# Attention scores as float32 products of q and k as loaded, with two buffers each for the loads of k and v

## The chip, the cores and the metric

The kernel runs on one core of one Trainium2 chip. The metric is the device time of one execution in microseconds; the median of three runs is quoted. The trace is one further execution, recorded by the hardware profiler.

## What is computed

An attention layer with a compressive memory, and behind it a feed-forward block (FFN) with a squared ReLU. `B, H, S, D = 4, 8, 576, 64`, so 2304 tokens of width 512; the hidden width is 2048. All inputs are float32.

```python
scores = where(causal, -1e9, q @ k.T / sqrt(D))
a = softmax(scores);  local = a @ v
q_p = phi(q)                                   # phi(x) = where(x > 0, x, exp(x) - 1) + 1
mem_out = (q_p @ M_prev) / (q_p @ z_prev + 1e-6)
g = sigmoid(beta)                              # one for each head
x = (g * mem_out + (1 - g) * local)            # heads side by side: 2304 x 512
out = (maximum(x @ w_in, 0) ** 2) @ w_out      # the FFN
```

## The kernel before

**The work.** The first 64 tokens of each batch are done together at the start (`first_tokens`). The remaining 512 queries of a batch are four tiles of 128 rows (tiles 1 to 4). A *unit* is one batch, one pair of heads and a list of tiles: batches 0 and 1 are cut into a low half (tiles 1, 2) and a high half (tiles 3, 4), batches 2 and 3 are not, which gives 24 units (0 to 23), numbered in the order in which they are traced. The 9 FFN blocks of 256 tokens are `moe(0)` to `moe(8)`; `moe(0)` has the first tokens, `moe(n)` a half of a batch. Attention outputs go to DRAM (`xd`, L567), and `prefetch` reads them back as `xn` (L588), transposes them (L591) and splits them into a rounded and a remainder part, `xh` and `xl`. The FFN multiplies with three float32r products for each pair of operands (L624 to L626, L614 to L616). The weights are loaded and split into `hi` and `lo` at the start (L160 to L166, loads in L190).

**A unit.** `loads` brings `kd` (both heads' k, transposed, 128 x 576), `qm` (memory matrix and q, two buffers) and `vv` (v), all on SP's queue. `kd` and `vv` have one buffer each (`KB`, `VVB`). For units 6 to 23, ScalarE (ACT) rounds q and k to float32r (`qh` L359, `kh` L364), and the remainders `ql` and `kl` are formed on VectorE (DVE) (L360, L365), or on GpSimd (POOL) for `kl` of units 6 to 11. The scores of a strip are then three products (`qh kh`, `ql kh`, `qh kl`) for each of the two heads, which lie on different halves of the array's rows. Units 0 to 5 (`NES`) multiply `qm` and `kd` themselves in float32; the trace shows two records for each such product. Strips have 192 (tile 1), 320 (tile 2), 448 (tile 3) and twice 288 columns (tile 4); tile 2 comes first (`TORD`). A single PSUM tile `sp` takes a strip of both heads. L465 on DVE adds the mask, writes `e` and takes the row minimum of the negated scores; L477 on ACT is the exponential. For units 0 and 1 the weights `e` are transposed on PE and multiplied with `vv` itself (L535). For all later units `e` is split into two float16 parts (L514, L516), transposed by a DMA (`aT`, L520) and multiplied with `vs` (L541 to L546). `vs` is `vv` scaled by a power of two that comes from its maximum `vx` (L393 to L403) and split into two float16 parts (L408, L410), after which `vv` is free.

**phi.** `pe`, the exponential of q, takes a slot of the ring `e` of three buffers. Units 6 to 23 write q's relu over q (L376) and join both on DVE (L377); units 0 to 5, whose q is still wanted by PE, take the minimum with 1 on POOL (L382) and join on DVE (L383). `pm` (L428) multiplies phi(q) with the memory matrix.

**The order of the work.** The program is traced unit by unit; next to the first four units stand the weights and `moe(0)`, and `moe(1)` to `moe(8)` are traced last. A scheduler of the language then orders each engine's instructions when the kernel is built: it takes the earliest traced instruction that its own model of time has ready, and allots the buffers. On the chip every engine and every DMA queue goes through its list in order, and instructions wait by semaphores. So the FFN matmuls fill PE where attention has nothing ready.

Of the kernel before, what the change touches and what calls it, by code (L numbers as in the profile page):

```python
# [8 lines left out]
F32 = mybir.dt.float32  # L9
F32R = mybir.dt.float32r  # L10
# [3 lines left out]
AF = mybir.ActivationFunctionType  # L14
ALU = mybir.AluOpType
AX = mybir.AxisListType

B, H, S, D = 4, 8, 576, 64
# [3 lines left out]
P = 128  # L22
# [6 lines left out]
SQ = S - D  # L29
# [4 lines left out]
SC = 16384.0  # L34
VEXP = 14
VL = 'dd'
PM = 'pd'
FX = 'dd'
GHN = 4
VMIN = 2.0**-80  # L40
NEF = 2
NES = 6
PXT = 'up'
PXE = 'aa'
PHI = 1
QB = 2
VVB = 1
ZW = D + 1
MW = 576
WSC = 1.0 / 256.0  # L50
EB = 3
RB = 1
KB = 1
XB = 2
PJ = 6
SEQ = 'a0 b0 g a1 r b1 r c0 l r r c1'
W0 = 9
EARLY = 'dp'
LATE = 'dd'
NEARLY = 12  # L60
SEG = 2
TORD = [2, 1, 3, 4]
# [25 lines left out]
def fused_kernel(ctx: ExitStack, tc: tile.TileContext, t0_d, zt_d, kk_d, qv_d, beta, w_in, w_out, out):  # L88
    nc = tc.nc
# [3 lines left out]
    at = ctx.enter_context(tc.tile_pool(name="at", bufs=1))  # L93
# [13 lines left out]
        out=mask, in_=mask, pattern=[[-1, MW]], compare_op=ALU.is_ge, fill=-1e30, base=448, channel_multiplier=1  # L107
# [219 lines left out]
    dp = ctx.enter_context(tc.tile_pool(name="dp", bufs=1, space=bass.MemoryType.DRAM))  # L327
# [12 lines left out]
        nc.sync.dma_start(vv[:, :nv], qv_d[b, p, :, SQ + 2 * ZW : SQ + 2 * ZW + nv])  # L340
        return kd, qm, vv

    def attention(b, p, tiles, ld, after, early, sfull, full):
        q_eng, k_eng = (nc.gpsimd if c == 'p' else nc.vector for c in (EARLY if early else LATE))
        late = 0 if early else 1
        h0 = 2 * p
        tl = tiles[-1]
        kn, ncn = sum(QT[tl]), tl + 1
        qa, qb = QT[tiles[0]][0] - D, kn - D
        kd, qm, vv = ld  # L350
        q_raw = qm[:, 2 * ZW :]
        mz = qm[:, : 2 * ZW]
        v = vv.rearrange("p (c x) -> p c x", c=5)
        heads = [slice(h * D, (h + 1) * D) for h in range(2)]

        if not sfull:
            qh, ql = (at.tile([P, SQ], F32R, tag=t, name=t) for t in ("qh", "ql"))
            kh, kl = (at.tile([P, S], F32R, tag=t, name=t) for t in ("kh", "kl"))
            nc.scalar.copy(qh[:, qa:qb], q_raw[:, qa:qb])  # L359
            q_eng.tensor_tensor(  # L360
                out=ql[:, qa:qb], in0=q_raw[:, qa:qb], in1=qh[:, qa:qb].bitcast(F32), op=ALU.subtract
            )
            yield
            nc.scalar.copy(kh[:, :kn], kd[:, :kn])  # L364
            k_eng.tensor_tensor(out=kl[:, :kn], in0=kd[:, :kn], in1=kh[:, :kn].bitcast(F32), op=ALU.subtract)  # L365
            yield
            terms = [(qh, kh), (ql, kh), (qh, kl)]
        else:
            terms = [(q_raw, kd)]

        pe = at.tile([P, 2, S], F32, tag="e", name="pe", bufs=EB)[:, 0]
        w = slice(qa, qb)
        nc.scalar.activation(pe[:, w], q_raw[:, w], AF.Exp)
        ph = pe if sfull else q_raw
        if PHI and not sfull:
            nc.scalar.activation(q_raw[:, w], q_raw[:, w], AF.Relu)  # L376
            nc.vector.scalar_tensor_tensor(  # L377
                out=q_raw[:, w], in0=pe[:, w], scalar=1.0, in1=q_raw[:, w], op0=ALU.min, op1=ALU.add
            )
        else:  # L380
            m_eng = nc.gpsimd if PM[late] == "p" else nc.vector
            m_eng.tensor_scalar(out=pe[:, w], in0=pe[:, w], scalar1=1.0, scalar2=None, op0=ALU.min)  # L382
            nc.vector.scalar_tensor_tensor(  # L383
                out=ph[:, w], in0=q_raw[:, w], scalar=0.0, in1=pe[:, w], op0=ALU.max, op1=ALU.add
            )
        yield

        if not full:
# [11 lines left out]
                out=vy, in0=vy, scalar1=VMIN, scalar2=2.0**-VEXP, op0=ALU.max, op1=ALU.mult  # L400
# [6 lines left out]
            if VL[late] == "d":  # L407
                nc.scalar.activation(vh, vr, AF.Copy, scale=vy)  # L408
                for h in range(2):
                    nc.vector.scalar_tensor_tensor(  # L410
                        out=vl[:, h], in0=vr[:, h], scalar=vy, in1=vh[:, h], op0=ALU.mult, op1=ALU.subtract
# [8 lines left out]
        for grp in (tiles[:2], tiles[2:]):  # L420
# [4 lines left out]
            for j, i in enumerate(grp):  # L425
# [6 lines left out]
                out=nm[:, :ng], in0=pv[:, :, :, D], scalar=1e-6,  # L432
# [14 lines left out]
        for i in [t for t in TORD if t in tiles]:  # L447
# [8 lines left out]
            for s in range(ns):  # L456
                ks = slice(s * w, (s + 1) * w)
                sps = ps.tile([P, 2, 512], F32, tag="s", name="sp")
                for x, (qt, kt) in enumerate(terms):
                    for h, hd in enumerate(heads):  # L460
                        nc.tensor.matmul(  # L461
                            sps[:n, h, :w], qt[hd, qc], kt[hd, ks], start=x == 0, stop=x == len(terms) - 1
                        )
                for h in range(2):
                    nc.vector.tensor_tensor_reduce(  # L465
                        out=e[:n, h, ks],
                        in0=sps[:n, h, :w],
                        in1=mask[:n, 448 - q0 + s * w : 448 - q0 + s * w + w],
                        scale=-0.125,
                        scalar=3e38 if s == 0 else mx[:n, h, 0:1],  # L470
                        op0=ALU.add,
                        op1=ALU.min,
                        accum_out=mx[:n, h, s : s + 1],
                    )
# [229 lines left out]
    def attn(i0, i1):  # L704
        for i in range(i0, i1):
            ld = nxt.pop()

            def after():
                if i + 1 < len(order):
                    nxt.append(loads(*order[i + 1]))  # L710

            yield from attention(*order[i], ld, after, i < NEARLY, i < NES, i < NEF and max(order[i][2]) < 4)

    def na(t):
        return NP * (6 + (len(t) > 3) + 2 * len(t) - 1)
# [64 lines left out]
```

## Time and profile before

| | |
|---|---|
| median of 3 runs | 610.11 us (610.11 to 610.82) |
| profiled execution: time, span | 609.23 us, 607.4 us |
| PE busy (matmul) | 569.1 us, 94% |
| DVE, ACT, POOL busy | 411.2 us (68%), 329.0 us (54%), 170.3 us (28%) |
| mean granted TensorE clock | 0.986 of full speed |
| chain that ended last | PE 63%, DVE 13%, DMA 9%, ACT 9% |

The span runs from the first to the last instruction, and the execution's time lies around it. PE's busy time is made of modelled matmul durations that overlap, so a busy PE is not PE at its peak; what a matmul costs is better read from the distance between starts.

### The profile page before, as it was taken

What the parts mean: (1) busy time and instruction counts of PE and PEld (TensorE: products, weight loads), DVE (VectorE), ACT (ScalarE), POOL (GpSimd) and SP (SyncE); (2) the same over time, 40 slices, a digit from 0 to 9 for tenths busy, and PEclk for the clock granted to TensorE, in tenths of its full rate; (3) what the DMA queues carried; (4) which work ended last, traced back from release to release, by engine and by line L of the source; (5) the groups of instructions that cost most, each with busy time, mean ns of one, the idle gap of its engine ahead of it and who ended that gap; (6) DMA issues with size and microseconds to landing.
All of it is one profiled execution on the core that took longest, in us unless ns stands there. A gap on an engine that the chain in (4) does not pass through costs nothing.

```text
span 607.4 us, 11542 instructions
## 1 busy us (share of the span) xinstructions
PE 569.1 (94%) x4198; PEld 482.7 (79%) x4198; DVE 411.2 (68%) x1285; ACT 329.0 (54%) x747; POOL 170.3 (28%) x139
## 2 busy tenths in 40 slices
PE   2479997999989999999999999999999999999997
PEld 2358876787868787888888888888888899998996
DVE  5999798868677879887888978788697711001000
ACT  3689686756566664775576645654556413312312
POOL 2501232134423233233332233232321121221221
PEclk9989998999997999999999999999999999999999
DMA  8947575673574775664655564575435510100000
GB/s 278 402 144 301 165 210 159 139 169 85 117 165 111 160 155 129 145 173 88 164 115 114 145 126 107 114 167 118 103 70 119 99 24 2 68 1 1 36 1 35
DMA packets 127576, 76.28 MB, mean 126 GB/s; under 512 B 99360, under 2 KB 112672, under 8 KB 127520
## 3 DMA queue, kind: packets, MB, share of 16 engines
q1 hardware_dynamic: 127520, 75.55, 49.7%
q8 instruction: 33, 0.54, 0.4%
q14 instruction: 23, 0.19, 0.1%
HBM read 42.63 MB, written 8.78 MB: 85 GB/s over the span
## 4 chain that ended last, share of the span: by engine, by line
PE 63%; DVE 13%; DMA 9%; ACT 9%; issue 3%; SPq 1%; POOL 1%; ACTq 0%
PE up L624 9%; PE up L626 8%; PE up L625 8%; PE oacc L614 8%; PE oacc L616 8%; PE oacc L615 8%; PE sp L461 6%; DMA aT<-a 3%; DMA vv<-in_qv_dram 3%; ACT e L477 2%; PE acc L546 2%; DVE a L516 2%; PE pm L428 2%; DVE e L465 2%; DVE memx L556 2%
## 5 line engine op out<-in xcount | busy, mean ns | idle before, releaser
L624 PE MATMUL up<-xh,w 128*128 128x256 f32 x576 | 167.0, 290 | 3.4 <-ACT aF L496 2.5
L626 PE MATMUL up<-xh,w 128*128 128x256 f32 x576 | 166.1, 288 | 0.0
L625 PE MATMUL up<-xl,w 128*128 128x256 f32 x576 | 165.9, 288 | 0.0
L639 POOL TENSOR_TENSOR gl<-r,gh 128x512 fp32r<-128x512 f32 x72 | 98.9, 1373 | 203.6 <-DVE gh L638 124.4
L624 PEld LDWEIGHTS up<-xh,w 128*128 128x128 f32 x576 | 111.2, 193 | 10.9 <-issue 3.9
L614 PE MATMUL oacc<-w,gh 128*128 128x512 f32 x288 | 116.0, 403 | 3.6 <-ACT gh L636 3.5
L625 PEld LDWEIGHTS up<-xl,w 128*128 128x128 f32 x576 | 111.3, 193 | 5.2 <-issue 2.5
L615 PE MATMUL oacc<-w,gh 128*128 128x512 f32 x288 | 114.4, 397 | 0.0
L626 PEld LDWEIGHTS up<-xh,w 128*128 128x128 f32 x576 | 111.2, 193 | 3.4 <-issue 2.2
L477 ACT ACTIVATE e<-e,mx 128x320 f32<-128x320 f32 (+3 forms) x128 | 77.8, 609 | 65.4 <-DVE mx L465 65.0
L616 PE MATMUL oacc<-w,gl 128*128 128x512 f32 x288 | 111.7, 403 | 0.0
L516 DVE SCALAR_TENSOR_TENSOR a<-e,a 128x128 f16<-128x128 f32 x120 | 79.4, 677 | 19.8 <-ACT a L514 19.6
L630 ACT ACTIVATE r<-up 128x512 f32<-128x512 f32 x72 | 42.4, 590 | 92.5 <-PE up L626 86.6
L632 POOL TENSOR_TENSOR r<-r 128x512 f32<-128x512 f32 x40 | 46.5, 1162 | 164.1 <-ACT r L630 164.1
L638 DVE CAST gh<-r 128x512 fp32r<-128x512 f32 x40 | 16.9, 423 | 87.9 <-ACT r L634 86.4
L614 PEld LDWEIGHTS oacc<-w,gh 128*128 128x128 f32 x288 | 54.5, 189 | 15.7 <-ACT gh L636 4.0
L616 PEld LDWEIGHTS oacc<-w,gl 128*128 128x128 f32 x288 | 53.2, 189 | 13.5 <-issue 3.8
L465 DVE CUSTOM_DVE_ANT_0 e<-sp,mask 128x320 f32<-128x320 f32 (+3 forms) x128 | 56.2, 475 | 9.0 <-PE sp L461 8.9
L615 PEld LDWEIGHTS oacc<-w,gh 128*128 128x128 f32 x288 | 54.5, 189 | 9.4 <-issue 0.9
L514 ACT ACTIVATE a<-e 128x128 f16<-128x128 f32 x120 | 56.9, 521 | 5.7 <-DMA aT<-a 4.7
L548 DVE TENSOR_REDUCE s<-acc 128x128 f32<-128x256 f32 x60 | 24.0, 417 | 21.2 <-PE acc L546 21.2
L546 PE MATMUL acc<-vs,aT 128*128 128x128 f16 x308 | 37.4, 222 | 0.0
(127 smaller groups left out, 883.4 us busy)
## 6 DMA issues: line engine op xcount, KB each, us to landing
raw<-in_w_in_dram SPq DMA_DIRECT2D x11, 512.0 KB, 7.9
vv<-in_qv_dram SPq DMA_DIRECT2D x16, 320.0 KB, 2.8
raw<-in_w_out_dram SPq DMA_DIRECT2D x9, 512.0 KB, 7.8
kd<-in_kk_dram SPq DMA_DIRECT2D x16, 288.0 KB, 3.1
out_dram<-o SPq DMA_DIRECT2D x16, 256.0 KB, 2.0
xd<-memx SPq DMA_DIRECT2D x31, 128.0 KB, 2.1
xn<-xd SPq DMA_DIRECT2D x14, 256.0 KB, 3.2
qm<-in_qv_dram SPq DMA_DIRECT2D x8, 321.0 KB, 2.9
```

Of the source, the lines that this page charges most:

```text
L465: nc.vector.tensor_tensor_reduce(out=e[:n, h, ks], in0=sps[:n, h, :w], in1=mask[:n, 448 - q0 + s * w : 448 - q0 + s * w + w], scale=-0.125 ...
L477: nc.scalar.activation(e[:n, h, :ke], e[:n, h, :ke], AF.Exp, bias=bs, scale=-1.0, accum_out=sm[:n, h : h + 1])
L514: nc.scalar.mul(av[:, :, o0 : o0 + w], x, SC)
L516: nc.vector.scalar_tensor_tensor(out=av[:, :, o0 + w : o0 + 2 * w], in0=x, scalar=SC, in1=av[:, :, o0 : o0 + w], op0=ALU.mult, op1=ALU.sub ...
L546: nc.tensor.matmul(o2, aT[:, h * nb + c, :n], vs[:, h, c], start=False, stop=c == i)
L614: nc.tensor.matmul(acc[t], gh[:, u, ts], w_out_op(f, 0), start=f == 0, stop=False)
L615: nc.tensor.matmul(acc[t], gh[:, u, ts], w_out_op(f, 1), start=False, stop=False)
L616: nc.tensor.matmul(acc[t], gl[:, u, ts], w_out_op(f, 0), start=False, stop=f == NF - 1)
L624: nc.tensor.matmul(up[:, u, :], w_in_op(f, k, 0), xh[:, k, :], start=k == 0, stop=False)
L625: nc.tensor.matmul(up[:, u, :], w_in_op(f, k, 0), xl[:, k, :], start=False, stop=False)
L626: nc.tensor.matmul(up[:, u, :], w_in_op(f, k, 1), xh[:, k, :], start=False, stop=k == NK - 1)
L639: nc.gpsimd.tensor_tensor(out=gl, in0=r, in1=gh.bitcast(F32), op=ALU.subtract)
```

## The change

All units multiply `q_raw` and `kd` in float32, so `qh`, `ql`, `kh` and `kl` go away with the four instructions that write them. phi is formed for all units from two tiles of its own, `ph` (two buffers) and `pr` (one), with exponential and relu on ACT and the join on DVE; `pe` no longer takes a slot of the ring `e`. `kd` and `vv` get a second buffer. The number of buffers of `qm` stays 2.

```diff
-VVB = 1
+VVB = 2
-KB = 1
+KB = 2
-        if not sfull:
-            qh, ql = (at.tile([P, SQ], F32R, tag=t, name=t) for t in ("qh", "ql"))
-            kh, kl = (at.tile([P, S], F32R, tag=t, name=t) for t in ("kh", "kl"))
-            nc.scalar.copy(qh[:, qa:qb], q_raw[:, qa:qb])
-            q_eng.tensor_tensor(
-                out=ql[:, qa:qb], in0=q_raw[:, qa:qb], in1=qh[:, qa:qb].bitcast(F32), op=ALU.subtract
-            )
-            yield
-            nc.scalar.copy(kh[:, :kn], kd[:, :kn])
-            k_eng.tensor_tensor(out=kl[:, :kn], in0=kd[:, :kn], in1=kh[:, :kn].bitcast(F32), op=ALU.subtract)
-            yield
-            terms = [(qh, kh), (ql, kh), (qh, kl)]
-        else:
-            terms = [(q_raw, kd)]
-
-        pe = at.tile([P, 2, S], F32, tag="e", name="pe", bufs=EB)[:, 0]
         w = slice(qa, qb)
-        nc.scalar.activation(pe[:, w], q_raw[:, w], AF.Exp)
...
+        ph = at.tile([P, SQ], F32, tag="ph", name="ph", bufs=2)
+        pr = at.tile([P, SQ], F32, tag="pr", name="pr", bufs=1)
+        nc.scalar.activation(ph[:, w], q_raw[:, w], AF.Exp)
+        nc.scalar.activation(pr[:, w], q_raw[:, w], AF.Relu)
+        nc.vector.scalar_tensor_tensor(
+            out=ph[:, w], in0=ph[:, w], scalar=1.0, in1=pr[:, w], op0=ALU.min, op1=ALU.add
+        )
...
-                for x, (qt, kt) in enumerate(terms):
-                    for h, hd in enumerate(heads):
-                        nc.tensor.matmul(
-                            sps[:n, h, :w], qt[hd, qc], kt[hd, ks], start=x == 0, stop=x == len(terms) - 1
-                        )
+                for h, hd in enumerate(heads):
+                    nc.tensor.matmul(sps[:n, h, :w], q_raw[hd, qc], kd[hd, ks], start=True, stop=True)
```

## Rows read from the trace of the kernel before

**Rows 1.** Busy time of each engine in four stretches of the span: stretch and its length, then busy us and instructions of PE, PE's weight loads, DVE, ACT and POOL, granted clock, DMA share and GB/s.

```profile
0.00:131.00 131.00, 102.97 (x728) 84.30 (x729) 113.01 (x329) 91.98 (x210) 33.20 (x32) 0.96 0.71 221
131.00:200.00 69.00, 64.39 (x490) 53.87 (x488) 54.12 (x185) 41.77 (x107) 26.18 (x22) 0.95 0.56 122
200.00:479.00 279.00, 276.96 (x2166) 231.45 (x2165) 228.85 (x736) 161.45 (x374) 82.94 (x65) 1.00 0.57 126
479.00:607.40 128.40, 124.80 (x821) 113.11 (x819) 15.19 (x37) 33.82 (x58) 27.94 (x22) 1.00 0.10 30
```

**Rows 2.** Waits of PE between 131 and 200 us: the instruction that waited, what it waited for, us in total, times, longest.

```profile
PE px L591 <- DMA xn<-xd: 2.1, 1, 2.1
PE acc L541 <- DMA aT<-a: 1.0, 1, 1.0
```

**Rows 3.** The stretch behind the read of `xn`, columns as in rows 1.

```profile
175.00:182.00 7.00, 4.33 (x42) 3.36 (x40) 5.72 (x25) 4.07 (x13) 0.86 (x1) 0.97 0.77 208
182.00:189.00 7.00, 6.89 (x34) 5.89 (x33) 5.50 (x25) 3.40 (x11) 0.00 (x0) 0.54 0.45 100
```

**Rows 4.** PE's instructions in order of time: whole groups of scores and the instruction behind each. `kd` operands are the float32 groups, `kh` and `kl` the float32r ones.

```profile
71.93 0.28 PE L626 MATMUL up<-xh,w 128*128 128x256 f32 x1
72.14 0.81 PE L461 MATMUL sp<-kd,qm 64*128 64x320 f32 x4
72.88 0.39 PE L624 MATMUL up<-xh,w 128*128 128x256 f32 x1
...
113.28 1.02 PE L461 MATMUL sp<-kd,qm 64*128 64x448 f32 x4
114.24 0.39 PE L624 MATMUL up<-xh,w 128*128 128x256 f32 x1
...
131.27 0.48 PE L461 MATMUL sp<-kh,qh 64*128 64x448 f32 x2
...
132.08 0.39 PE L625 MATMUL up<-xl,w 128*128 128x256 f32 x1
...
163.99 0.42 PE L461 MATMUL sp<-kh,qh 64*128 64x320 f32 x2
...
164.63 0.39 PE L624 MATMUL up<-xh,w 128*128 128x256 f32 x1
```

**Rows 5.** The scores' matmuls of L461, one term of the float32r groups: count, shortest, median and longest ns, first and last start, and the shapes.

```profile
L461 PE MATMUL sp<-kh,qh x132: 353/398/632, 131.3 to 477.3; 64*128 64x288 f32 x56, 64*128 64x448 f32 x28, 64*128 64x320 f32 x24, 64*128 64x192 f32 x24
```

**Rows 6.** PE's instructions in order of time: the first and the last of the 21 float32r groups that are cut by other work (the first between the heads, the last between the terms), and one of those between.

```profile
155.71 0.40 PE L461 MATMUL sp<-kh,qh 64*128 64x288 f32 x2
...
173.33 0.42 PE L461 MATMUL sp<-kh,qh 64*128 64x320 f32 x2
...
173.83 0.73 PE L616 MATMUL oacc<-w,gl 128*128 128x512 f32 x2
...
176.32 0.41 PE L461 MATMUL sp<-kl,qh 64*128 64x320 f32 x2
176.66 0.23 PE L541 MATMUL acc<-vs,aT 128*128 128x128 f16 x1
...
456.19 0.41 PE L461 MATMUL sp<-kh,qh 64*128 64x320 f32 x2
```

**Rows 7.** The same view: the one float32 group that is cut between its heads, first head.

```profile
87.48 1.02 PE L461 MATMUL sp<-kd,qm 64*128 64x448 f32 x2
88.43 0.50 PE L614 MATMUL oacc<-w,gh 128*128 128x512 f32 x1
```

**Rows 8.** Groups of instructions by line: count, busy us and mean ns of one, and the engine's idle time before them with what ended it.

```profile
L364 ACT CAST kh<-kd 128x576 fp32r<-128x576 f32 (+1 forms) x18 | 11.2, 622 | 28.2 <-PE sp L461 28.2
L376 ACT ACTIVATE qm<-qm 128x256 f32<-128x256 f32 (+1 forms) x18 | 9.0, 503 | 0.2 <-DVE ql L360 0.2
L359 ACT CAST qh<-qm 128x256 fp32r<-128x256 f32 (+1 forms) x18 | 8.9, 496 | 0.6 <-DMA qm<-in_qv_dram 0.6
L360 DVE TENSOR_TENSOR ql<-qm,qh 128x256 fp32r<-128x256 f32 (+1 forms) x18 | 13.2, 733 | 0.4 <-ACT qh L359 0.3
L365 DVE TENSOR_TENSOR kl<-kd,kh 128x576 fp32r<-128x576 f32 x12 | 9.0, 750 | 0.0
L365 POOL TENSOR_TENSOR kl<-kd,kh 128x320 fp32r<-128x320 f32 (+1 forms) x6 | 7.4, 1225 | 15.7 <-ACT kh L364 15.7
L382 POOL TENSOR_SCALAR pe<-pe 128x256 f32<-128x256 f32 x6 | 6.3, 1057 | 31.4 <-ACT pe L373 31.0 <-PE acc L535 0.4
```

**Rows 9.** The chain of work that ended last, in order of time: start, us, what.

```profile
142.87 3.28 DMA vv<-in_qv_dram
```

**Rows 10.** SP's queue in order of time, ahead of the read of `xn` for the second block: start, us of the issue, what.

```profile
175.95 0.52 SPq L340 DMA_DIRECT2D vv<-in_qv_dram  x1
...
177.00 0.90 SPq L588 DMA_DIRECT2D xn<-xd  x2
```

**Rows 11.** SP, ACT and PE in order of time around the last weight loads.

```profile
84.62 0.33 SPq L340 DMA_DIRECT2D vv<-in_qv_dram  x1
86.19 0.33 SPq L190 DMA_DIRECT2D hw<-in_w_out_dram  x1
...
90.80 0.69 ACT L161 ACTIVATE hw<-hw 128x512 f32<-128x512 f32 x1 [2.79 <-DMA hw<-in_w_out_dram]
...
101.91 0.50 PE L614 MATMUL oacc<-w,gh 128*128 128x512 f32 x1 [3.51 <-ACT gh L636]
```

More of the change, by code (lines that the diff above doesn't have):

```diff
@@ L36 @@
 VL = 'dd'
-PM = 'pd'
 FX = 'dd'
@@ L41 @@
 NEF = 2
-NES = 6
 PXT = 'up'
 PXE = 'aa'
-PHI = 1
 QB = 2
-VVB = 1
+VVB = 2
 ZW = D + 1
@@ L57 @@
 W0 = 9
-EARLY = 'dp'
-LATE = 'dd'
 NEARLY = 12
@@ L341, in loads, with attention @@
         return kd, qm, vv
-    def attention(b, p, tiles, ld, after, early, sfull, full):
-        q_eng, k_eng = (nc.gpsimd if c == 'p' else nc.vector for c in (EARLY if early else LATE))
+    def attention(b, p, tiles, ld, after, early, full):
         late = 0 if early else 1
@@ L354, in attention @@
         heads = [slice(h * D, (h + 1) * D) for h in range(2)]
-        if not sfull:
-            qh, ql = (at.tile([P, SQ], F32R, tag=t, name=t) for t in ("qh", "ql"))
-            kh, kl = (at.tile([P, S], F32R, tag=t, name=t) for t in ("kh", "kl"))
-            nc.scalar.copy(qh[:, qa:qb], q_raw[:, qa:qb])
-            q_eng.tensor_tensor(
-                out=ql[:, qa:qb], in0=q_raw[:, qa:qb], in1=qh[:, qa:qb].bitcast(F32), op=ALU.subtract
-            )
-            yield
-            nc.scalar.copy(kh[:, :kn], kd[:, :kn])
-            k_eng.tensor_tensor(out=kl[:, :kn], in0=kd[:, :kn], in1=kh[:, :kn].bitcast(F32), op=ALU.subtract)
-            yield
-            terms = [(qh, kh), (ql, kh), (qh, kl)]
-        else:
-            terms = [(q_raw, kd)]
-        pe = at.tile([P, 2, S], F32, tag="e", name="pe", bufs=EB)[:, 0]
-        w = slice(qa, qb)
-        nc.scalar.activation(pe[:, w], q_raw[:, w], AF.Exp)
[L374 to L378, printed above, removed]
-            )
[L380 to L385, printed above, removed]
+        w = slice(qa, qb)
+        ph = at.tile([P, SQ], F32, tag="ph", name="ph", bufs=2)
[5 more added lines that the diff above has]
+        )
         yield
@@ L458, in attention @@
                 sps = ps.tile([P, 2, 512], F32, tag="s", name="sp")
-                for x, (qt, kt) in enumerate(terms):
-                    for h, hd in enumerate(heads):
-                        nc.tensor.matmul(
-                            sps[:n, h, :w], qt[hd, qc], kt[hd, ks], start=x == 0, stop=x == len(terms) - 1
-                        )
+                for h, hd in enumerate(heads):
+                    nc.tensor.matmul(sps[:n, h, :w], q_raw[hd, qc], kd[hd, ks], start=True, stop=True)
                 for h in range(2):
@@ L710, in after @@
                     nxt.append(loads(*order[i + 1]))
-            yield from attention(*order[i], ld, after, i < NEARLY, i < NES, i < NEF and max(order[i][2]) < 4)
+            yield from attention(*order[i], ld, after, i < NEARLY, i < NEF and max(order[i][2]) < 4)
     def na(t):
```

## The prediction

> **What bounds the kernel now.** I read the busy shares by stage first [rows 1]. Until 131 us no engine is full: PE is busy 102.97 of 131 us, DVE 113.01. From 200 to 479 us PE is busy 276.96 of 279 us, and after that 124.80 of 128.4. So from 200 us on the time is the sum of PE's work: a microsecond added to PE there is a microsecond of the span, and one taken from DVE or ACT is worth nothing by itself. Between the two lies 131 to 200 us, where PE idles 4.6 us (69.00 less 64.39) although the FFN block has work queued. The waits of PE in that stretch name it: the read of the next block's tokens, `xn`, and the transposed weights `aT` [rows 2]. Behind the `xn` wait the granted clock fell too: 0.54 of full speed over the 7 us from 182 to 189 us, after PE had been busy for only 4.33 of the 7 us before, so some 3.2 us more of work were lost there ((1 - 0.54) x 7) [rows 3]. In all 7.8 us are to be had in this stretch, and 2.0 after it up to 479 us.
>
> **The fourth pass, on PE.** Units 0 to 5 already multiply in float32, units 6 to 23 with three float32r products, so both prices stand in the trace. I take a group (both heads of one strip of scores) from its first start to the start of the next instruction. With 320 columns float32 takes 72.88 - 72.14 = 0.74 us, with 448 columns 0.96; float32r takes 0.64 and 0.81 [rows 4]. Per column that is (0.96 - 0.74) / 128 = 1.7 ns against (0.81 - 0.64) / 128 = 1.3 ns; on these lines 288 columns cost 0.69 and 0.60, 192 columns 0.52 and 0.47. Units 6 to 23 have 66 groups: 12 with 192 columns, 28 with 288, 12 with 320, 14 with 448 [rows 5], the instructions of one term halved for the two heads. With whole groups on both sides the change adds 12 x 0.05 + 28 x 0.09 + 12 x 0.10 + 14 x 0.15 = 6.4 us.
>
> But the float32r groups aren't whole. Going through PE's timeline I count 21 of the 66 that are cut by other work, 18 of them between terms (scores start on `kh` and `qh`, and `kl` or `ql` comes later) and 3 between the heads; first and last stand in [rows 6]. A cut is dear, since every group has two edges: it starts 0.09 us late (71.93 + 0.12, the step of these matmuls, is 72.05, and the group starts at 72.14), and the matmul behind it lasts 0.39 instead of 0.28 [rows 4]. Edges are 0.20 us in all. The 320-column group at 173.33 takes 0.50 and, at 176.32, 0.34 more; against a whole one of 0.64 that is 0.20, and the second pair of edges makes 0.40 a cut. 21 x 0.40 = 8.4 us. Float32 operands come straight from the load, so there is no late term to cut at: only the cut between heads stays. One of the 14 float32 groups was cut so, and each head alone took 0.95 us [rows 7], as much as both together, so this cut costs 0.95 + 0.95 - 0.96 + 0.20 = 1.1 us. At 3 to 5 of 66 that is 3 to 6 us; I take 5. PE's sum: 6.4 - 8.4 + 5 = +3 us, between -2 (none cut) and +6.4 (the cuts of before come back in some other place, so that nothing is saved).
>
> The Trainium skill, in FP8 and Floating Point Precision (TensorE Precision Notes), says that true float32 goes through the array in four passes. The trace agrees, at 1.7 ns a column against 1.3 for three. By the pass count alone this speaks against the change; it is a rival below, and the sum here doesn't use it.
>
> **What goes from ACT, DVE and POOL.** Four instructions a unit for 18 units: the casts `kh` and `qh` (11.2 + 8.9 us of ACT), `ql` and `kl` (13.2 + 9.0 of DVE, 7.4 of POOL) [rows 8]. From 200 us on PE covers all of it, so I book nothing there. With `kh` goes ACT's wait for its single buffer: 28.2 us in which ACT stood until PE had done the last scores of the unit before [rows 8]. PE covers that too. The second exponent buffers `ph` and `pr` replace a slot of the `e` ring; the same PSUM and the same instructions on DVE remain. In units 0 to 5 POOL's minimum (6 x 1.06 us) becomes a relu on ACT; the nearest rows are the relu of the later units, 0.50 us a piece over both widths [rows 8], so up to 6 x 0.50 = 3.0 us if all six lie on the path, none if POOL's step was the longer way round. I take 0.5.
>
> **The second buffers.** A unit's `vv` may now be loaded before the unit before has scaled its own. At 142.87 us the chain of work that ended last goes through this load, 3.28 us [rows 9]; the load stood for the slot that VectorE frees, and in VectorE's order the maximum `vx` of the loaded tile stands ahead of an `a` and with it the `aT` transposes that PE waits for. Gone is thus one reload in each unit on the chain, and for units 6 and 7 the kl of POOL on top. SP's queue has the same wait in front of other work: the `xn` read was issued at 177.00 us, behind a `vv` load at 175.95 which stood for the scaling [rows 10]. Between them lies a `qm` load, which may keep some of the 1.05 us: it needs the last scores of two units earlier now, because `q` is read by PE itself; the transposes and the `xn` read queue behind it on SP, and PE waits for both. `pr` has one buffer, which VectorE frees after one instruction; I book nothing for it, since the next relu is a whole unit later. The second `kd` buffer buys nothing new: it stands in for `kh` and `kl`, since `kd` is now held until the last scores.
>
> What is that worth? At least nothing: `aT` (a DMA after the slowest DVE step) and the round trip of `xd` and `xn` stay. At most the 7.8 us. The attention of units 4 to 7 has to end some 4 us earlier for PE not to run dry; two reloads of about 3 us and the split of units 6 and 7 are more than that, if VectorE follows. I take 5.5 of the 7.8.
>
> Before 131 us `vv` loads stand ahead of weight loads in SP's queue as well: issued at 84.62, followed by a weight load at 86.19 for which ACT then waits 2.79 us at 90.80, and PE stands 3.51 us at 101.91 for ACT [rows 11]. So 0 to 3.5 us; DVE is busy almost throughout, so I take 1.5.
>
> **Sum.** 3 (PE) + 0.5 (relu) - 5.5 (131 to 200 us) - 1.5 (early) = -3.5 us. The profiled execution has a span of 607.4 us and a time of 609.23; 605.7 for this one's time. The median of the runs shown is 610.11, 0.9 above it, so I predict 606.6.
>
> **The rivals.**
> *A: the fourth pass is paid and nothing comes back* (slower). The extra pass counts on PE after 200 us, where nothing hides it, at 6.4 us, and the stall before the second block only changes its name: `aT` and `xn` are still late, because DVE, not the load, sets them. Plus the relu, 0 to 3: 616.5 to 619.5; with half of the stalls recovered 613. For it: PE is 99% busy there. Against it: 21 cuts are in the rows, and their cause is removed. It decides where PE's extra is larger than the stalls recovered. Counted in passes alone the price is higher: one more for 20,480 columns (12 x 192 + 28 x 288 + 12 x 320 + 14 x 448) at 1.3 / 3 = 0.43 ns is 8.9 us, and 610.11 + 8.9 = 619. The Trainium skill's FP8 and Floating Point Precision gives this count. The whole groups of [rows 4] lie less far apart than that, 0.10 us at 320 columns where a pass is 0.14. Together 0.27.
> *B: no difference* (608.9 to 611.3). Stalls of 3 us recovered and 3 us of extra passes, or the wait of `vv` replaced by that of `qm`, which has two buffers and is held longer: 0.14. That the second buffers do nothing because SP's order puts the loads late again belongs here.
> *C: the large gain.* No float32 group is cut (-2), the 7.8 us come back whole and the early stand of 3.5 too: 597 to 602. For it: each of the three is in the rows. Against it: the scheduler lays out the whole order anew. 0.17.
>
> **Chances.** My case (602 to 608.9) 0.42, A 0.27, B 0.14, C 0.17. Faster by over 0.2% (1.2 us, about what a measurement here can tell from no change) thus 0.59, within it 0.14, slower 0.27. The range that leaves out no more than 2 in 10: 599 to 616.5; my case's own is 602 to 608.9.
>
> **What would show it.** (1) Groups at L461's place with two `kd` records a head and 0.69 us at 288 columns; cuts only between heads, fewer than 6 of 66. (2) 131 to 200 us: PE idle below 2 us and no clock below 0.9. (3) DVE's wait of `vx` for `vv` gone, ACT's for `kh` gone, with no change of PE's share after 200 us. (4) An `xn` read for the second block that is issued before 174 us. I am wrong if cut float32 groups are many, if PE gets a new wait in the early stage, or if the stall before the second block stays although `vv` is early: then DVE set it.

## The result, and the profile after

The changed kernel takes 618.57 us (median, 616.58 to 619.24) where the kernel before, on the same chip, takes 610.47. The ratio is 1.0127, with a 95% interval of 1.0101 to 1.0153: slower by 1.3%. The profiled execution has a span of 616.2 us against 607.4.

The stretches of the changed kernel, with the columns of [rows 1]:

```profile
0.00:131.00 131.00, 100.27 (x689) 82.15 (x690) 109.56 (x310) 89.85 (x206) 28.02 (x25) 0.92 0.66 212
131.00:200.00 69.00, 66.63 (x485) 53.84 (x483) 55.35 (x184) 39.98 (x99) 18.26 (x15) 0.95 0.61 134
200.00:279.00 79.00, 73.72 (x540) 58.47 (x539) 65.86 (x212) 44.30 (x101) 19.82 (x16) 1.00 0.72 152
279.00:479.00 200.00, 198.71 (x1501) 161.52 (x1500) 154.86 (x524) 106.83 (x257) 58.13 (x48) 1.00 0.57 119
479.00:616.20 137.20, 133.58 (x861) 121.24 (x858) 13.33 (x30) 33.69 (x57) 30.31 (x24) 1.00 0.07 25
```

Between 131 and 200 us PE idles 2.4 us (69.00 - 66.63) where it idled 4.6: part of the gain that was forecast. Before that, PE does 100.27 us of work instead of 102.97, at a granted clock of 0.92 instead of 0.96. And between 200 and 279 us, a stretch in which I had booked nothing, it now idles 5.3 us; before, the whole of 200 to 479 us had 2.0 us of idle time. To put these on one scale I priced every matmul in both timelines by its steady step (0.12 us for `up`, 0.23 for `oacc`, and so on) and compared when the same sum of work was reached. The changed kernel is some 6 us late at 126 us of the old time, 2 to 3 late at 210, 7 to 8 late at 255, and between 6 and 10 from there to the end (these figures move by a microsecond or two with the prices chosen; the spans end 8.8 apart). So it loses twice, early and at 210 to 255 us, and regains some 4 between.

PE's waits in the second of these stretches, 200 to 279 us (who waited for what; us in total, times, longest):

```profile
PE acc L510 <- DVE vs L382: 2.0, 2, 1.7
PE sp L432 <- DVE mx L434: 1.1, 2, 0.7
PE vt L369 <- DVE s L517: 1.0, 1, 1.0
PE acc L510 <- DMA aT<-a: 0.6, 1, 0.6
PE sp L432 <- DMA qm<-in_qv_dram: 0.4, 1, 0.4
```

Most of it, 4.1 of the 5.1 us listed, is for DVE. The instructions of several engines there, in order of time (start, us, engine, what; in brackets the idle time before it and what ended it):

```profile
208.93 0.81 DVE L365 TENSOR_REDUCE vx<-vv 128x1 f32<-128x640 f32 x1
...
217.83 1.45 DVE L382 SCALAR_TENSOR_TENSOR vs<-vv,vy,vs 128x192 f16<-128x192 f32 x2
...
219.34 0.33 SPq L335 DMA_DIRECT2D vv<-in_qv_dram  x1
...
222.90 0.82 DVE L365 TENSOR_REDUCE vx<-vv 128x1 f32<-128x640 f32 x1 [1.89 <-DMA vv<-in_qv_dram]
...
224.29 0.22 PE L369 MATMUL vt<-identb,vx 128*128 128x128 bf16 x1 [1.01 <-DVE s L517]
...
225.82 0.78 ACT L446 ACTIVATE e<-e,mx 128x576 f32<-128x576 f32 x1 [6.43 <-DVE mx L434]
...
230.90 2.02 DVE L382 SCALAR_TENSOR_TENSOR vs<-vv,vy,vs 128x320 f16<-128x320 f32 x2
...
232.51 0.22 PE L510 MATMUL acc<-vs,aT 128*128 128x128 f16 x1 [1.70 <-DVE vs L382]
...
258.06 2.04 DVE L382 SCALAR_TENSOR_TENSOR vs<-vv,vy,vs 128x320 f16<-128x320 f32 x2
```

The second buffer is there, but the order of the lists uses it up. The load at 219.34 follows at once the scaling (217.83) that frees its buffer, and DVE waits 1.89 us for it before the `vx` at 222.90, although the scaling that needs this `vx` comes only at 258.06; the scaling at 230.90 belongs to the `vx` of 208.93. Behind the waiting `vx` in DVE's list are `s`, which PE waits for, and the row maxima `mx`, for which ACT has waited 6.43 us. With one buffer DVE waited for a load that it needed next; with two it waits for one that it needs a unit later.

### The profile page after: what moved, and what is told of

It reads as the page before. It is cut to its first block, busy times and chain, and to the rows that moved or that the text cites. A ratio compares the mean times of both kernels' runs of the same rounds, so it can differ in the third digit from the quotient of the medians.

```text
span 616.2 us, 11137 instructions
## 1 busy us (share of the span) xinstructions
PE 572.9 (93%) x4066; PEld 477.2 (77%) x4066; DVE 399.0 (65%) x1255; ACT 314.7 (51%) x717; POOL 154.5 (25%) x127
## 4 chain that ended last, share of the span: by engine, by line
PE 62%; DVE 15%; DMA 10%; ACT 6%; issue 4%; SPq 1%; POOL 1%; ACTq 0%; DVEq 0%; POOLq 0%
PE up L593 9%; PE up L595 9%; PE up L594 9%; PE oacc L583 8%; PE oacc L584 8%; PE oacc L585 8%; PE sp L432 6%; DMA raw<-in_w_in_dram 4%; ACT e L446 3%; DVE a L485 3%; DMA aT<-a 2%; DVE e L434 2%; PE acc L515 2%; DVE memx L525 2%; DMA vv<-in_qv_dram 2%
## 5 line engine op out<-in xcount | busy, mean ns | idle before, releaser
L593 PE MATMUL up<-xh,w 128*128 128x256 f32 x576 | 169.5, 294 | 0.9 <-DVE xl L566 0.7
L594 PE MATMUL up<-xl,w 128*128 128x256 f32 x576 | 168.9, 293 | 0.0
L595 PE MATMUL up<-xh,w 128*128 128x256 f32 x576 | 168.7, 293 | 0.0
L593 PEld LDWEIGHTS up<-xh,w 128*128 128x128 f32 x576 | 113.7, 197 | 9.7 <-issue 5.6
L594 PEld LDWEIGHTS up<-xl,w 128*128 128x128 f32 x576 | 113.8, 198 | 7.7 <-issue 5.4
L595 PEld LDWEIGHTS up<-xh,w 128*128 128x128 f32 x576 | 113.6, 197 | 6.3 <-issue 5.6
L485 DVE SCALAR_TENSOR_TENSOR a<-e,a 128x128 f16<-128x128 f32 x120 | 83.1, 703 | 24.4 <-ACT a L483 23.6
L601 POOL TENSOR_TENSOR r<-r 128x512 f32<-128x512 f32 x40 | 44.9, 1123 | 204.2 <-ACT r L599 200.6
L432 PE MATMUL sp<-kd,qm 64*128 64x288 f32 (+3 forms) x320 | 68.6, 486 | 17.9 <-DVE mx L434 9.9
L432 PEld LDWEIGHTS sp<-kd,qm 64*128 64x128 f32 x320 | 26.2, 191 | 33.7 <-DVE mx L434 13.8
```

Of the source, the lines that this page charges most:

```text
L432: nc.tensor.matmul(sps[:n, h, :w], q_raw[hd, qc], kd[hd, ks], start=True, stop=True)
L485: nc.vector.scalar_tensor_tensor(out=av[:, :, o0 + w : o0 + 2 * w], in0=x, scalar=SC, in1=av[:, :, o0 : o0 + w], op0=ALU.mult, op1=ALU.sub ...
L593: nc.tensor.matmul(up[:, u, :], w_in_op(f, k, 0), xh[:, k, :], start=k == 0, stop=False)
L594: nc.tensor.matmul(up[:, u, :], w_in_op(f, k, 0), xl[:, k, :], start=False, stop=False)
L595: nc.tensor.matmul(up[:, u, :], w_in_op(f, k, 1), xh[:, k, :], start=False, stop=k == NK - 1)
```

## The experiments

A name that begins with a is the changed kernel with an edit, one with b the kernel before with an edit. All ratios are to the kernel before on the same chip. The runs are from several chips, on which the kernel before takes 609.76 to 610.47 us, so a difference between two runs in microseconds can be off by up to 0.7 us from this alone.

### Is it the fourth pass?

**b_nes24**: the kernel before with float32 scores in all units. `NES` also decides the form of phi: units 6 to 23 now take the minimum too, on POOL in units 6 to 11 and on DVE behind that, in place of ACT's relu.

```diff
-NES = 6
+NES = 24
```

> The kernel before with the first part alone: all units multiply q and k as loaded in float32, one buffer each for kd and vv, phi as units 0 to 5 form it in the kernel before (minimum with 1, then a join; on POOL up to unit 11, on DVE behind that), with its exponent still in the ring e. Theory P (the fourth pass on PE is what makes the changed kernel slow): 616 to 619. Theory N (PE's price is neutral, 64.3 against 63.6 us by the traces; the loss comes from what else moved): 607 to 613, with a span in which PE's work behind 131 us is within 2 us of that of the kernel before. Theory O (the loss is in how DVE's and ACT's lists come to be ordered, whichever part is made): no sum over parts holds, and anything between 604 and 618 may come; a loss, if there is one, stands as idle PE time before 260 us.

Measured: 609.79 us, ratio 0.9988 [0.9964, 1.0011]. Float32 scores, with the four instructions for rounded parts and remainders gone and with this form of phi, cost nothing that can be measured.

**a_twice**: units 6 to 23 of the changed kernel issue every group of scores twice. This is the price of PE time by itself.

```diff
-                for h, hd in enumerate(heads):
-                    nc.tensor.matmul(sps[:n, h, :w], q_raw[hd, qc], kd[hd, ks], start=True, stop=True)
+                for _ in range(1 + twice):
+                    for h, hd in enumerate(heads):
+                        nc.tensor.matmul(sps[:n, h, :w], q_raw[hd, qc], kd[hd, ks], start=True, stop=True)
```

> The changed kernel in which units 6 to 23 issue each group of float32 score products twice (the second overwrites the first, so the scores are the same). It measures whether PE's time for scores reaches the span one to one. A group's matmuls without edges take 0.32 us at 192 columns (4 passes of 80 ns), 0.48 at 288, 0.53 at 320, 0.75 at 448, in all 34 us for 66 groups, 48 us with the edge that stands in a group's time. If PE bounds (all theories on the price of passes need it): 652 to 668 us. If PE's stands have room for it: below 640 us.

Measured: 664.88 us, 46.3 more than the changed kernel, of 48 priced. Work that is added to PE does reach the end almost one to one, so the premise of [rows 1] holds. By the traces the fourth pass costs nothing because the pieces are fewer: the 66 groups of units 6 to 23 stand on PE in 87 pieces before and in 69 after. From first start to next start they take 46.3 us before and 49.8 after (five pieces that met a stall or the half clock counted at the usual time of their kind), and with 0.20 us of edges a piece it is 46.3 + 17.4 = 63.7 against 49.8 + 13.8 = 63.6. The expectation of b_nes24 has 64.3 and 63.6, by a count of 70 pieces after that took in one of unit 5. A whole group of 288 columns of the changed kernel, and one of the three of 66 that are cut between their heads:

```profile
159.38 0.76 PE L432 MATMUL sp<-kd,qm 64*128 64x288 f32 x4
160.06 0.38 PE L593 MATMUL up<-xh,w 128*128 128x256 f32 x1
...
268.00 0.75 PE L432 MATMUL sp<-kd,qm 64*128 64x288 f32 x2
268.68 0.23 PE L510 MATMUL acc<-vs,aT 128*128 128x128 f16 x1
...
269.63 0.75 PE L432 MATMUL sp<-kd,qm 64*128 64x288 f32 x2
270.31 0.50 PE L583 MATMUL oacc<-w,gh 128*128 128x512 f32 x1
```

160.06 - 159.38 = 0.68 us for both heads, and each head alone takes the same 0.68.

### Is it the second buffers?

**a_vv1** (`VVB = 1`) and **a_vv1kb1** (also `KB = 1`): the changed kernel without them.

```diff
-VVB = 2
+VVB = 1
-KB = 2
+KB = 1
```

> The changed kernel with one buffer for vv (VVB 1) and everything else as changed. Theory W (the loss comes from the order of the instruction lists: VectorE stands for vv loads that it does not need yet, and PE stands behind it between 205 and 255 us): the maximum vx of a unit can no longer run a unit ahead, and some 4 us of the 8 come back, 613 to 615 us. Rival P (the fourth pass of the float32 scores is what costs): no difference from the changed kernel, 617.5 to 619.5 us. Third theory, the one of the forecast (one buffer makes PE wait at the second block): slower than the changed kernel, 621 to 624 us.

> The changed kernel with one buffer each for kd and vv: scores in float32 and the new phi alone. Theory B (the second buffers give nothing in this kernel): 616 to 620, as with both. Theory K (kd, now held until the last scores, needs its second buffer): slower than with both by more than 2 us, above 620.5. Theory O: may as well be faster than with both buffers, below 616, if the shorter look-ahead of vv on DVE's list falls better.

Measured: 617.82 us, ratio 1.0123 [1.0066, 1.0181], and 617.13 us, 1.0102 [1.0076, 1.0128]. Within these intervals (a_vv1's is 7 us wide) the buffers neither cause the loss nor give anything here.

**b_vv2**: the kernel before with `VVB = 2`.

> The kernel before with a second buffer for vv alone (VVB 2), scores still as three float32r products. The forecast's step: stands before the second block go, 604 to 607 us. Theory W: the buffer moves vx a unit ahead in VectorE's list and VectorE stands for loads as before: no gain, 610 to 614 us. Rival P says nothing on it beyond that it stays well below the changed kernel (618).

Measured: 605.39 us, ratio 0.9933 [0.9907, 0.9959]. In the order of the kernel before the second `vv` buffer is worth 5.1 us. A second `kd` buffer wasn't tried there.

**a_vxhold**: the changed kernel, with `vx` queued on DVE behind the last scaling of the unit before.

```diff
-            nc.vector.tensor_reduce(out=vx, in_=vc, axis=AX.XY, op=ALU.max, apply_absolute_value=True)
+            with tc.issue_after(held[0].ins) if held else nullcontext():
+                nc.vector.tensor_reduce(out=vx, in_=vc, axis=AX.XY, op=ALU.max, apply_absolute_value=True)
...
-                    nc.vector.scalar_tensor_tensor(
+                    held[:] = [nc.vector.scalar_tensor_tensor(
...
```

> The changed kernel, in which the maximum vx of a unit is queued on VectorE behind the last scaling of the v of the unit before (order only, no wait), so that the load that the second buffer allows is some 12 us old when VectorE reads it. Theory W: VectorE's waits for vv loads vanish and with them most of PE's stands between 205 and 255 us: 613 to 615 us. Rival P: 617.5 to 619.5 us, although the waits for vv are gone.

Measured: 610.88 us, ratio 1.0000 [0.9977, 1.0023], 7.7 us off the changed kernel, a larger gain than the expected 613 to 615. DVE no longer waits for `vv` at all between 60 and 480 us (9.5 us in the changed kernel), and PE is full from 200 to 279 us:

```profile
200.00:279.00 79.00, 78.75 (x569) 62.30 (x568) 60.79 (x200) 46.18 (x102) 21.86 (x18) 1.00 0.66 152
```

The profiled execution took 607.98 us. On the scale of summed work above it doesn't lose the 5 us that the changed kernel loses between 210 and 255 us, and is some 4 us ahead of it at 126 us already; what the edit changes in the order of the lists there I haven't traced.

**b_vv2_hold**: b_vv2 with the same edit.

> The kernel before with two vv buffers (605.4 us) and vx queued on VectorE behind the scaling of the unit before. Theory W (VectorE's stands for loads cost PE time in any such kernel; 19 us of them in the run with two buffers): 598 to 603 us. Theory S: 603 to 612 us, no rule to be seen, although VectorE's waits for vv go.

Measured: 604.36 us, ratio 0.9901 [0.9872, 0.9930], 1.0 us off b_vv2, which is less than its interval. In b_vv2 DVE waited 19.1 us for `vv` in 60 to 480 us, twice as long as in the changed kernel, and taking these waits away gained next to nothing. So the length of such waits says little; what counts, I take it, is what stands behind them.

### Is it phi in units 0 to 5?

**a_phi**: the changed kernel, with units 0 to 5 taking the minimum on POOL as before instead of the relu on ACT.

`early` is 2 in units 0 to 5; behind the lines shown, the relu and its join follow for the other units as they were.

```diff
+        if early == 2:
+            nc.gpsimd.tensor_scalar(out=ph[:, w], in0=ph[:, w], scalar1=1.0, scalar2=None, op0=ALU.min)
+            nc.vector.scalar_tensor_tensor(
+                out=ph[:, w], in0=q_raw[:, w], scalar=0.0, in1=ph[:, w], op0=ALU.max, op1=ALU.add
+            )
...
```

> The changed kernel with phi of units 0 to 5 as before, the minimum on GpSimd in place of the relu on ACT (still in the tile ph). Theory E (the early part lost its 4 us between 50 and 60 us because ACT got the relus): 613 to 616 us. If the early loss is a matter of order, not of these six relus: within 2 us of the changed kernel, 616.5 to 620.5 us. Rival P: no difference either.

Measured: 611.97 us, ratio 1.0019 [1.0001, 1.0037]: 6.6 us off the changed kernel, a larger gain than the expected 613 to 616. DVE waits 19.0 us for `vv` between 60 and 480 us here, against 9.5 in the slower changed kernel.

**a_phi_hold** (this and the hold of `vx`) and **a_phi_kb1** (this with `KB = 1`):

> The changed kernel with both edits that helped: the minimum on GpSimd for phi of units 0 to 5 (612.0 us alone) and vx queued behind the scaling of the unit before (610.9 us alone). If the two repair two separate places (early part and 205 to 255 us), they add up: 618.6 - 6.6 - 7.7 = 604 us, 602 to 607. If each merely shook the order of the lists into another of many like ones (theory S), they don't add up: 608 to 615 us.

> As the changed kernel with phi of units 0 to 5 as before, and with one buffer for kd (KB 1): next to the kernel before with two vv buffers (605.4 us) this has float32 scores and the tiles ph and pr. kd is held until the last scores of its unit, so the next load (3 us) and the scores behind it wait for them. Theory K (the second kd buffer is needed as a stand-in for kh and kl): 614 to 622 us, slower than with two (612.0). If the load is hidden by other tiles' work: 610 to 614 us.

Measured: 601.86 us, ratio 0.9866 [0.9829, 0.9903], and 613.75 us, 1.0033 [1.0002, 1.0065]. The two edits add up, and a little more (6.6 and 7.7 us alone, 16.7 together); together they make the fastest kernel here, with float32 scores and both second buffers. By the medians the second `kd` buffer is worth 1.8 us; the intervals overlap, so it may be nothing.

**b_relu**: the kernel before with this part of the change alone.

```diff
-        if PHI and not sfull:
+        if sfull:
+            pr = at.tile([P, SQ], F32, tag="pr", name="pr", bufs=1)
+            nc.scalar.activation(pr[:, w], q_raw[:, w], AF.Relu)
+            nc.vector.scalar_tensor_tensor(
+                out=pe[:, w], in0=pe[:, w], scalar=1.0, in1=pr[:, w], op0=ALU.min, op1=ALU.add
+            )
+        elif PHI and not sfull:
```

> The kernel before with the phi part alone: units 0 to 5 form the relu on ACT in a tile of its own and join it on DVE, instead of the minimum on POOL; everything else as before. Theory E (each of these six ACT operations, about 0.5 us, delays the exponentials behind it in the stretch where ACT and DVE are full): slower by 2 to 7 us, 612 to 617, with the lag made before 110 us. Theory O (only the order of the lists matters): no such sign; within 3 us of 610.5 to either side, or a gain.

Measured: 622.35 us, ratio 1.0188 [1.0160, 1.0216]. This part alone costs 12 us, more than the whole change, but not where it was expected: on the scale of summed work b_relu is within some 2.5 us of the kernel before from 57 to 210 us of the old time; it loses 8 us up to 255 and 5 more between 345 and 395, where I haven't followed it. Its instructions around 230 us:

```profile
222.09 1.52 SPq L337 DMA_DIRECT2D qm<-in_qv_dram  x2
...
225.09 0.81 SPq L594 DMA_DIRECT2D xn<-xd  x2
...
225.52 0.47 PE L467 MATMUL sp<-kh,qh 64*128 64x448 f32 x2
...
226.07 0.33 SPq L340 DMA_DIRECT2D vv<-in_qv_dram  x1
...
230.45 0.82 DVE L399 TENSOR_REDUCE vx<-vv 128x1 f32<-128x640 f32 x1 [4.86 <-DMA vv<-in_qv_dram]
...
233.64 0.62 DVE L471 CUSTOM_DVE_ANT_0 e<-sp,mask 128x448 f32<-128x448 f32 x1
...
234.86 0.40 PE L467 MATMUL sp<-kh,qh 64*128 64x288 f32 x2 [2.19 <-DVE mx L471]
```

The single `vv` buffer is reloaded at 226.07, behind a `qm` load and an `xn` read on SP's queue. DVE waits 4.86 us for it, its list behind that is late, and PE waits 2.19 us for the instruction that forms the row maxima: that one reads the strip `sp`, whose single tile PE fills next.

The Trainium skill, in PSUM — Partial Sum Buffer (Engine vs sequencer instructions), says that VectorE's queue is strictly first in, first out. This trace agrees: the mask instruction at 233.64, whose scores PE began at 225.52, starts only behind the waiting `vx` of 230.45.

**b_relu_vv2_hold**: b_relu with the second `vv` buffer and the hold.

> The kernel before with the phi part (alone 622.35), two buffers for vv and vx queued behind the last scaling of the unit before (these two without the phi part 604.36). Theory V (the phi part loses because in its order DVE stands for the load of vv where PE is short; with the load early and vx last, that wait is gone): 603 to 608. Theory F (the phi part costs its 12 us by another way): 614 to 618.

Measured: 609.38 us, ratio 0.9980 [0.9959, 1.0000], 13.0 us off b_relu. That was just outside the 603 to 608 expected, and 5 us above b_vv2_hold; most of the 12 us went, not all. The buffer and the hold weren't tried apart here. From 200 to 260 us, b_relu and then b_relu_vv2_hold:

```profile
200.00:260.00 60.00, 52.91 (x387) 44.44 (x386) 43.12 (x139) 31.89 (x74) 15.38 (x12) 0.94 0.52 118
```

```profile
200.00:260.00 60.00, 60.00 (x437) 49.76 (x436) 48.37 (x151) 33.41 (x74) 17.29 (x14) 0.97 0.59 133
```

### The relu that is there, or the minimum that isn't?

**a_norelu**: the changed kernel without the six relus (`pr = q_raw` in units 0 to 5, so the relu is left out of their phi and nothing takes its place). **a_both**: the changed kernel with the six relus on ACT and six minima on POOL, which nothing needs. The two lines of a_both ahead of the join:

```diff
+            nc.scalar.activation(pr[:, w], q_raw[:, w], AF.Relu)
+            nc.gpsimd.tensor_scalar(out=ph[:, w], in0=ph[:, w], scalar1=1.0, scalar2=None, op0=ALU.min)
...
```

> The changed kernel without the relu of units 0 to 5: the join there adds q itself, so their phi is wrong for negative q; the six ACT operations are left out and nothing takes their place. Theory E (the six operations cost by being on ACT): as fast as with the minimum on POOL or a little faster, 609 to 612.5. Theory O (the gain of the minimum on POOL was a different order of the lists): not tied to 612; as near to 618 as to 610.

> The changed kernel with both steps in units 0 to 5: the relu on ACT stays, and the minimum on POOL is added ahead of the join (the join takes the minimum once more, which changes nothing). With the relu alone 618.57, with neither 619.46, with the minimum alone 611.97. Theory J (the minimum makes the join ready later, and so gives it a later place in DVE's list; the ACT operations don't matter): 610 to 614. Theory E (the ACT operations cost): 617 to 621. Theory O (nothing but chance in the order): between them or outside of both.

Measured: 619.46 us, ratio 1.0136 [1.0095, 1.0176], and 611.87 us, 1.0013 [0.9989, 1.0037]. The four kernels make a square: relu alone 618.57, neither 619.46, minimum alone 611.97, both 611.87. Six operations less on ACT gain nothing; six superfluous operations more on POOL gain 6.7 us. In these four kernels they go with a later place of the join in DVE's list. The joins of units 0, 1 and 2 in the changed kernel, a_norelu, a_phi and a_both, in this order:

```profile
18.68 0.90 DVE L355 SCALAR_TENSOR_TENSOR ph<-ph,pr 128x256 f32<-128x256 f32 x1
...
25.97 0.99 DVE L355 SCALAR_TENSOR_TENSOR ph<-ph,pr 128x256 f32<-128x256 f32 x1
...
44.06 0.42 DVE L355 SCALAR_TENSOR_TENSOR ph<-ph,pr 128x256 f32<-128x256 f32 x1
```

```profile
17.71 0.90 DVE L358 SCALAR_TENSOR_TENSOR ph<-ph,qm 128x256 f32<-128x256 f32 x1
...
24.45 0.41 DVE L358 SCALAR_TENSOR_TENSOR ph<-ph,qm 128x256 f32<-128x256 f32 x1
...
43.09 0.42 DVE L358 SCALAR_TENSOR_TENSOR ph<-ph,qm 128x256 f32<-128x256 f32 x1 [0.83 <-ACT ph L353]
```

```profile
22.38 0.41 DVE L356 SCALAR_TENSOR_TENSOR ph<-qm,ph 128x256 f32<-128x256 f32 x1
...
27.42 0.40 DVE L356 SCALAR_TENSOR_TENSOR ph<-qm,ph 128x256 f32<-128x256 f32 x1
...
54.59 1.51 DVE L356 SCALAR_TENSOR_TENSOR ph<-qm,ph 128x256 f32<-128x256 f32 x1
```

```profile
22.06 0.41 DVE L357 SCALAR_TENSOR_TENSOR ph<-ph,pr 128x256 f32<-128x256 f32 x1
...
27.09 1.26 DVE L357 SCALAR_TENSOR_TENSOR ph<-ph,pr 128x256 f32<-128x256 f32 x1
...
52.78 0.42 DVE L357 SCALAR_TENSOR_TENSOR ph<-ph,pr 128x256 f32<-128x256 f32 x1
```

Two and two alike, as their times are. In the two slow ones the join of unit 2 is at 44.06 and 43.09 us, in the fast ones at 54.59 and 52.78, which is 22 or 23 instructions later in DVE's list.

The kernel before and b_relu don't show such a move. The join of unit 2 in the kernel before, b_relu and b_relu_u0 (the next runs below), in this order:

```profile
55.27 0.72 DVE L383 SCALAR_TENSOR_TENSOR pe<-qm,pe 128x256 f32<-128x256 f32 x1
```

```profile
53.53 0.42 DVE L378 SCALAR_TENSOR_TENSOR pe<-pe,pr 128x256 f32<-128x256 f32 x1
```

```profile
54.05 0.70 DVE L389 SCALAR_TENSOR_TENSOR pe<-qm,pe 128x256 f32<-128x256 f32 x1
```

In b_relu the join of unit 0 comes nine instructions earlier than in the kernel before and those of units 1 to 5 at most three; in b_relu_u0 the first moves by the same nine. Yet b_relu loses 12 us and b_relu_u0 nothing. So the place of the early joins alone doesn't account for b_relu.

**a_phi_u0**, **a_phi_u5** and **b_relu_u0**: a_phi with the minimum in unit 0 or unit 5 alone, b_relu in unit 0 alone.

> The changed kernel with the minimum on POOL for unit 0 alone (all of units 0 to 5 gave 611.97 against 618.57). Theory E (each of the six has its price): a sixth of 6.6 us, 617 to 618. Theory O (any small edit has the order of the lists laid anew, and the time follows from where waits then fall): not tied to a sixth; a change of 3 us or more to either side is as likely as not, and the lag against the changed kernel is made behind 130 us, long after unit 0.

> The changed kernel with the minimum on POOL for unit 5 alone. Theory E: 617 to 618, as for unit 0. Theory O: as for unit 0, and not the same time as that one; a difference of 3 us or more between the two.

> The kernel before with the relu on ACT for unit 0 alone (all of units 0 to 5 gave 622.35 against 610.37). Theory E: a sixth of 12 us, 612 to 613. Theory O: anything from 605 to 622, with the lag made far from unit 0.

Measured: 618.46 us, ratio 1.0120 [1.0090, 1.0151]; 617.58 us, 1.0120 [1.0093, 1.0147]; and 610.92 us, 1.0010 [0.9994, 1.0026]. One unit moves nothing much either way, so in these three cases a small edit didn't throw the order at random, as one of the theories had it. It takes several units. For a_phi a sixth of the whole effect (1.1 us) would fit as well as nothing; for b_relu a sixth would be 2.0 us, and the interval ends at 1.6.

**b_nes24_vv2_hold**: the kernel before with float32 scores, the second `vv` buffer and the hold.

> The kernel before with float32 scores in all units (alone 609.79), two buffers for vv, and the maximum vx queued on DVE behind the last scaling of the unit before (these two alone 604.36); one buffer for kd, phi as units 0 to 5 form it. Theory N (float32 scores neutral, the hold takes away most of what the order can spoil): 602 to 606. Theory P (float32 scores cost on PE): 609 or more. Theory O without more: any value from 600 to 612.

Measured: 607.35 us, ratio 0.9926 [0.9896, 0.9957]. It beats the kernel before, though by less than the 602 to 606 expected. By the medians it doesn't reach b_vv2_hold (604.36) or a_phi_hold (601.86), but the intervals overlap.

## Why the prediction was wrong

It said 606.6 us, and the kernel takes 618.57. By its own steps:

- **The premise** (from 200 us on, the time is the sum of PE's work) held for work that is added: a_twice. But the sentence drawn from it, that nothing need be booked for DVE and ACT there, failed. PE was 99% busy there because DVE's list happened to serve it in time; with the lists of the changed kernel it idles 5.3 us from 200 to 279 us, with those of a_vxhold, for the same work, 0.3 (79.00 - 78.75).
- **The fourth pass**, +3 us (between -2 and 6.4): the run shows -0.6 with an interval of -2.2 to +0.7 us (610.37 x 0.0036 and 0.0011). It holds a change of phi in units 6 to 23 too, but the count of pieces, 63.7 against 63.6 us, says the same. Cuts between heads are 3 of 66, at 0.88 us each (0.68 and 0.20 of edges), so 2.6 us where I booked 5, and the cuts that go away pay for the pass. Point (1) came true, with 0.68 us.
- **The relu**, +0.5 us (0 to 3.0): this is the step that failed. I priced six operations by their durations and booked nothing for what the edit does to the lists of the other engines. Alone it costs 12.0 us (b_relu), in the changed kernel 6.6 (a_phi), and in the latter not through ACT's operations: without them nothing is gained (a_norelu), with POOL's minimum back the loss is gone although they stay (a_both). What I had written as the case of no loss, "if POOL's step was the longer way round", missed that a step which goes away can also move the instruction behind it forward in another engine's list, as it does in the changed kernel.
- **131 to 200 us**, -5.5 us: PE's idle time fell by 2.2 of the 4.6 us, and the lag shrank by 4 from 126 to 210 us; but points (2) and (4) weren't met: the `xn` read is issued at 180.45 us, against 177.00 in [rows 10], the transposes start at 182.96, against 180.80, and the clock behind them falls as in [rows 3] (last section). On SP's queue the read now follows the write of `xd` at 178.43, not a `vv` load, so the attention in front of it ends no earlier; that DVE sets its end is likely, but not shown. [rows 2] also leaves out PE's second longest wait in this stretch, 1.2 us for the row maxima, which the second view here gives; the first is of the changed kernel.

```profile
180.45 0.33 SPq L557 DMA_DIRECT2D xn<-xd  x1
...
182.96 0.54 PE L560 MATMUL px<-identr,xn 128*128 128x128 f32 x4 [0.77 <-DMA xn<-xd]
```

```profile
PE sp L461 <- DVE mx L465: 1.2, 2, 0.8
```

- **The second buffers**: in the order of before `vv`'s is worth 5.1 us, near the 5.5 + 1.5 forecast; in the changed kernel nothing that can be measured (a_vv1). So of the 7.0 us booked, none is left at the end, and this is about as large a part of the miss as the relu. Of point (3), ACT's wait for `kh` is gone, but `vx` still waits for `vv`, 9.5 us between 60 and 480 us against 13.4 before, and PE's share after 200 us fell.
- **Rival A** gave the right sign and nearly the right time, 616.5 to 619.5, for a reason that b_nes24 and the count of pieces refute: that is luck. The Trainium skill, in FP8 and Floating Point Precision (TensorE Precision Notes), gives the four passes from which the prediction estimated 619. No run here shows that price, since the float32 groups replace cut ones.

Alone, the parts measure -0.6 (scores), +12.0 (phi of units 0 to 5) and -5.1 (`vv`), 616.7 from 610.4 in all. The second `kd` buffer and the tiles `ph` and `pr` in units 6 to 23 weren't tried alone. That the sum comes near 618.57 is in part chance, as the parts are worth other amounts in each other's company.

**What stays open.** The square shows that POOL's minimum in units 0 to 5 decides in the changed kernel, and not ACT's relu; that it does so by the place of the joins fits the four traces, but no join was held back without a minimum, and b_relu doesn't bear it out. That DVE's waits for `vv` pass a loss on to PE at 210 to 255 us is borne out by a_vxhold, and by b_relu_vv2_hold as far as buffer and hold go together; both edits also lay the lists anew. a_both idles as long as the changed kernel between 200 and 260 us (PE is busy 54.68 of 60 us) and has its lead of some 4 us over it by 57 us, of 4.6 at the end of the span. So the minimum saves time early and the hold later. By which steps the order of the first 100 us leads to b_relu's loss behind 210 us I haven't shown.

## What to carry to other kernels

When a scheduler orders the engines' lists, price a removed or moved step twice: its duration, and what its result's earlier readiness may do to the list of the engine behind it. A second buffer for a load can be worth 5.1 us in one order of the lists and nothing in another. Where the first reader of that load stands in its engine's list ahead of work that is due sooner, try to hold that reader back: this was worth 7.7 us in the changed kernel with no operation saved, and 1.0, within the noise, in b_vv2. Try such parts one by one: a gain and a loss of the same change hid each other here.

## What the runs showed of the hardware

Early on, the granted clock cost about as much as the stalls before it. Around 112 us PE of the changed kernel waits twice for DVE:

```profile
111.76 0.76 PE L432 MATMUL sp<-kd,qm 64*128 64x288 f32 x4 [1.37 <-DVE mx L434]
113.23 0.58 PE L593 MATMUL up<-xh,w 128*128 128x256 f32 x1 [0.71 <-DVE xl L566]
```

Behind that the granted clock is near half, until 119 us. Stretches of 5 us from 110, 115 and 185 us, columns as in [rows 1]:

```profile
110.00:115.00 5.00, 2.92 (x16) 2.27 (x16) 5.00 (x14) 1.61 (x4) 0.00 (x0) 0.75 0.49 115
115.00:120.00 5.00, 5.00 (x28) 5.00 (x28) 1.06 (x6) 2.78 (x7) 0.00 (x0) 0.57 0.62 145
...
185.00:190.00 5.00, 4.86 (x25) 3.92 (x25) 4.63 (x19) 2.91 (x9) 0.00 (x0) 0.50 0.56 52
```

From 115 to 120 us PE is busy throughout and does 28 matmuls. The kernel before did 44 in the same stretch, at 1.00 of full speed:

```profile
115.00:120.00 5.00, 5.00 (x44) 4.22 (x44) 4.67 (x16) 3.70 (x10) 1.29 (x1) 1.00 0.75 148
```

In the rows of single matmuls, `up` steps by 0.21 us until 119.2 and by 0.12 from 119.4 on: the two levels, 1.2 and 2.4 GHz. The 27 steps from 113.23 to 119.16 took 5.9 us, where 0.12 us each would make 3.2; the two waits are 2.1 us. At 185.25 a whole group of 320 columns takes 1.37 us to the next start, where it is 0.74 in [rows 4].
